# Attention into two mixture layers: the fp16 high parts written by ScalarE, and a router chain cut into eleven pieces

## Chip, cores and metric

The kernel runs on one core of a Trainium2 chip. The metric is device time in microseconds (us) of one execution; three executions of the kernel before gave a median of 1026.43 us (1021.26 to 1030.29).

## What is computed

The reference first runs a chunked attention over 4 batches, 8 heads, 768 positions and head size 64: each chunk of 32 queries sees its own 32 keys, 16 to the left, 8 to the right and 8 memory keys. The result, 3072 tokens of width 512, goes through a top-2 mixture of 8 experts with a noisy router, and then through a top-1 mixture of 8 other experts:

```
scores = 0.125 * q_c @ k_full.T ; a = softmax(scores) ; out[c] = a @ v_full
noisy = x @ w_gate + log1p(exp(x @ w_noise)) * noise
top2 = two largest of noisy ; weights = softmax over the two
out[token] += weight[k] * relu(x @ w1[e]) @ w2[e]       for its two experts e
second mixture: the one expert of largest logit, weight = softmax probability
```

## The kernel before

The tokens are worked in 24 tiles of 128 tokens (t = 0 to 23, `NT`). The attention loop in `build` (lines 1253 to 1302) runs 26 rounds, and the program gives each engine its instructions exactly in the order in which this loop writes them; each engine works its own queue in that order, and semaphores hold an instruction until its data is there. In round t the loop writes:

- `scores(t)`, lines 305 to 326: 32 matmuls `s` on TensorE (PE, L316), then on VectorE (DVE) a maximum `m` (L323) and a subtraction `d` (L325).
- `flip(t-1)`, lines 335 to 342: four transposes `pt` on PE, copied by ScalarE (ACT) into `et`.
- `exp(t)`, lines 328 to 333: three activations on ACT.
- pieces of the router chain, lines 1280 to 1282 (below).
- `values(t-2)`, lines 344 to 376: 32 matmuls `o` on PE (L356), then on DVE `r`, its reciprocal and the product `x` (L362, L363, L365), the fp16 cast of `x` (L369), which is the high part; GpSimd (POOL) subtracts to make the low part (L370). Both parts are stored to `X16` by a DMA on SyncE's queue (SP), behind the five loads of tile t+3 (L293).
- `spread(t)`, lines 295 to 303: two or four copies on POOL that fill the neighbour rows of the value tile.
- `turn(t-3)`, lines 378 to 384: eight transposes `xp` on PE of the two parts, copied by ACT into `xt` (L384).
- `logits(t-4)`, lines 386 to 392: eight small matmuls `lg` on PE.

The accumulators `o`, `pt` and `xp` have one buffer each, `s` has two; so `o(t-2)` can't start before DVE has finished `x(t-3)`, and `xp(t-3)` can't start before ACT has copied `xp(t-4)`. Five tile buffers (`LK`) hold the loaded inputs: the load of tile t+3 waits until PE has finished `o(t-2)`.

After every sixth tile the router of that batch is worked by the generator `route` (lines 394 to 495), whose `yield`s cut it into pieces; each `next(route)` writes one piece. Its parts are named here A (logits, exp, ln), B (noise, maximum of eight and its index, L408 to L419), C (one-hots, L422 to L436), D (`count` on PE, positions, L438 to L452), E (one-hot tables on DVE, L454 to L461), F (table matmuls on PE, L465, then table and gates, L467 to L484) and G (L487 to L494, middle batches only). A batch's chain begins at the end of rounds 9, 15 and 21; the fourth batch's chain is run in `tail()` by the `Driver`, one piece per step of the first mixture.

From round 14 on, 512 KB weight chunks are loaded ahead (`Weights`, four `stage` buffers). Rounds 24 and 25 each convert one chunk: ACT writes the fp16 high part (`high`, L127), DVE the low part (`low`, L128). Two more chunks follow (c0 to c3 in all) before the first expert's matmuls `ph` (L543) can run to the end of their first output tile. The first mixture then runs 15 groups of two or three tiles, with matmuls `ph` and `py` (L543, L554).

Of the kernel before, what the change touches and what calls it, by code (L numbers as in the profile page):

```python
# [10 lines left out]
AF = mybir.ActivationFunctionType  # L11
# [11 lines left out]
DM, F, E = 512, 1024, 8  # L23
# [199 lines left out]
def count(nc, g, pos, cnt, oh, carry=None):  # L223

    n = oh.shape[1]
    last = carry is None
    nc.tensor.matmul(pos, g.tri, oh, start=True, stop=False)
    for s in range(1, n):
        nc.tensor.matmul(pos[:, s:, :], g.ones, oh[:, :n - s, :], start=False, stop=last and s == n - 1)
    if not last:  # L230
        nc.tensor.matmul(pos, g.ones, carry[:, None, :].to_broadcast([128, n, E]), start=False, stop=True)
    if cnt is not None:
        for t in range(n):
            nc.tensor.matmul(cnt, g.ones, oh[:, t, :], start=(t == 0), stop=(t == n - 1))
# [20 lines left out]
class Attention:  # L255
# [88 lines left out]
    def values(self, t):  # L344
        nc, wk, g = self.nc, self.wk, self.g
        x = self.X[t % LK]
        y = self.ET.pop(t)
        o = self.ps.tile([128, 2, 512], F32, name="o")
        for a in range(2):
            for u in range(2):  # L350
                for ch in range(4):
                    i = (D + 1) * (4 * ch + 2 * a + u)
                    v = x[:, i:i + D + 1]
                    v = bass.AP(tensor=v.tensor, offset=v.offset, ap=[v.ap[0], [XV + (3 - 2 * ch) * VC, 2], v.ap[1]])
                    j = 64 * (ch % 2) + 32 * u
                    nc.tensor.matmul(o[32 * ch:32 * ch + 32, a, 130 * u:130 * u + 130],  # L356
                                     y[:, 2 * (ch // 2) + a, j:j + 32], v, start=True, stop=True)
        if t + LK < NT:
            self.load(t + LK)
        o = o[:, :, 0:260].rearrange("p a (h d) -> p a h d", h=4)  # L360
        r = wk.tile([128, 2, 4, 1], F32, name="r")
        nc.vector.tensor_scalar(r, o[:, :, :, D:D + 1], 1e-9, 1.0 / SX, op0=OP.add, op1=OP.mult)  # L362
        nc.vector.reciprocal(r, r)  # L363
        x = wk.tile([128, 2, 4, D], F32, name="x", bufs=2)
        nc.vector.tensor_tensor(x, o[:, :, :, 0:D], r.to_broadcast([128, 2, 4, D]), op=OP.mult)  # L365
        xp = x.rearrange("p b a d -> p (b a d)")
        w = g.rr.tile([128, 2, 4, 128], F16, name="x16", bufs=2)
        wf = w.rearrange("p a k q -> p (a k q)")
        nc.vector.tensor_copy(wf[:, :DM], xp)  # L369
        nc.gpsimd.tensor_tensor(wf[:, DM:], xp, wf[:, :DM], op=OP.subtract)  # L370
        y = self.XT[t] = g.rr.tile([128, 2, 4, 128], F16, name="xt", bufs=3)
        if t >= NT - 2:
            nc.sync.dma_start_transpose(out=y.rearrange("p a k q -> p (a k) q"), in_=wf)
        else:
            self.W[t] = w
        self.stores.append(nc.sync.dma_start(rows(g.X16, t), wf))
# [17 lines left out]
    def route(self, b):  # L394

        nc, g = self.nc, self.g
# [15 lines left out]
        i8 = rr.tile([128, TB, 8], U32, name="i8")  # L412
        for j in range(TB):
            V.max(m8[:, j, :], ny[:, j, :])
        for j in range(TB):
            V.max_index(i8[:, j, :], m8[:, j, :], ny[:, j, :])
        dd = rr.tile([128, TB, 2], F32, name="dd")
# [8 lines left out]
                        op=OP.is_equal)  # L426
        two = rr.tile([128, TB, E], F16, name="two")
        V.tensor_tensor(two, oh[:, :, 0, :], oh[:, :, 1, :], op=OP.add)

        vb = rr.tile([128, TB, 2], F32, name="vb")  # L430
        vr = rr.tile([128, TB, 2], F32, name="vr")
# [6 lines left out]
        pp = g.psr.tile([128, 512], F32, name="misc")  # L438
        p3 = pp[:, 0:TB * E].rearrange("p (t e) -> p t e", t=TB)
        count(nc, g, p3, None, two, g.carry)  # L440
        pr = rr.tile(sh, F32, name="pr")
        V.tensor_tensor(pr, oh, p3[:, :, None, :].to_broadcast(sh), op=OP.mult)
        pos = g.pos[:, ts, :]
        with nc.allow_low_precision("positions are integers"):
# [15 lines left out]
        ol, ov = onehots(nc, g, lo.rearrange("p t k -> p (t k)"), col.rearrange("p t k -> p (t k)"), g.slot,  # L460
                          eng=None)  # L461
        yield 6.5
        tp = pp[:, 128:128 + NC]
        for i in range(M):
            nc.tensor.matmul(tp, ol[:, :, i], ov[:, :, i], start=(i == 0), stop=(i == M - 1))  # L465
# [6 lines left out]
        V.tensor_tensor(full, full, tp, op=OP.add)  # L472
        V.tensor_tensor(gt[:, :, 1], gt[:, :, 0], dd[:, :, 0], op=OP.mult)
        V.tensor_tensor(g.T, g.T, full, op=OP.add)
        if b:

            n = NC if b == B - 1 else max(k // 128 + 8 * u for u, k in enumerate(LEAST[b]) if k)
            g.tabs.append(tables1(nc, g.c, g.T, n, f"t{b}"))
# [35 lines left out]
def rows(x, t):  # L514

    return x.rearrange("(u p t) d -> u p t d", u=2, t=M)[t // M, :, t % M]


def tables1(nc, pool, T, n, name, mem=None):

    V = nc.vector
    v, gi, xi, yi = mem or [pool.tile([128, n], F32 if u == "v" else I32, name=name + u) for u in "vgxy"]
    T = T[:, 0:n]
    V.tensor_scalar(gi, T, -1.0, 0.0, op0=OP.add, op1=OP.max)
    V.tensor_scalar(xi, gi, 1, None, op0=OP.arith_shift_right)
    V.tensor_scalar(v, T, 0.0, float(BIG), op0=OP.is_equal, op1=OP.mult)
    V.tensor_tensor(yi, gi, v, op=OP.add)
    return xi, gi, yi
# [686 lines left out]
def build(tc, xa, xb, xc, xd, xe, noise, wr, wg2, w1, w2, v1, v2, out):  # L1215
    nc = tc.nc
    with ExitStack() as top:
# [18 lines left out]
        def src(e):  # L1236
            v = (w1[e].rearrange("(p k) f -> p (k f)", k=4), w2[e].rearrange("(p k) d -> p (k d)", k=8))
            return lambda i, c: v[i][:, c * 1024:c * 1024 + 1024]

        with ExitStack() as ctx:  # L1240
            wk = ctx.enter_context(tc.tile_pool(name="wk", bufs=2))
            ld = ctx.enter_context(tc.tile_pool(name="ld", bufs=1))
            at = Attention(tc, g, (xa, xb, xc, xd, xe), ld, wk)
            at.ps = ctx.enter_context(tc.tile_pool(name="psa", bufs=1, space=PSUM))
            at.load(0)
            nc.scalar.preload_act_table_set("natural_log_exp_and_others")
            gates = at.gates(noise, wr)
            at.clear(0)
            constants(tc, g, ld)
            for t in range(1, LK):  # L1250
                at.load(t)
            route = None
            for t in range(NT + 2):
                if t + 1 < LK:
                    at.clear(t + 1)
                if t == 0:
                    next(gates)
                if t == 3:
                    at.wrh = next(gates)
                if t == 2:  # L1260
                    g.wide = g.c.tile([128, 128, M], F16, name="wide")
                    nc.vector.tensor_copy(g.wide, g.iota[:, 0:128, None].to_broadcast([128, 128, M]))
                    z = ld.tile([128, NT * E], F32, name="zero")
                    nc.vector.memset(z, 0.0)
                    for u in range(2):
                        nc.sync.dma_start(g.L.rearrange("(u p t) x -> u p (t x)", u=2, p=128)[u], z)
                    nc.sync.dma_start(g.G.rearrange("(p t) x -> p (t x)", p=128), z[:, 0:2 * NT])
                if t >= 14:
                    W.depth = min(W.depth + 1, 4)
                    if t == 14:  # L1270
                        for e in range(E):
                            W.add((1, e), src(e))
                    W.fill()
                if t < NT:
                    at.scores(t)
                if 0 < t <= NT:
                    at.flip(t - 1)
                if t < NT:
                    at.exp(t)
                if route and t < 25:  # L1280
                    for _ in range(2 if t in (17,22) else 1):
                        next(route, None)
                if t >= 2:
                    at.values(t - 2)
                if t < NT:
                    at.spread(t)
                if 0 <= t - 3 < NT - 2:
                    at.turn(t - 3)
                if t >= 4:
                    at.logits(t - 4)  # L1290
                if t >= 4 and (t - 4) % TB == TB - 1:
                    route = at.route((t - 4) // TB)
                    next(route)
                if t == 20:
                    m1 = Moe1(tc, g, dr)
                    m1.gather(0)
                if t == 22:
                    for b in range(m1.preps(0)):
                        m1.prep(0, b)
                if t >= 24 and W.may():  # L1300
                    W.high()
                    W.low(nc.vector)
            m1.gates(0)
# [224 lines left out]
```

## Time and profile before

| what | value |
| --- | --- |
| median of three runs | 1026.43 us |
| lowest, highest | 1021.26, 1030.29 us |
| the profiled execution | 1026.23 us |
| its span, first to last instruction | 1024.4 us |
| PE busy | 961.8 us, 94% |
| DVE, ACT, POOL busy | 498.4, 383.9, 480.8 us |

The span is 1.8 us shorter than the profiled execution's own time, and that execution is 0.2 us below the median. Times inside the program are counted from the start of the span. The shares are means over the whole program: PE is busy nearly all the time in the two mixtures, which begin near 147 us, while the attention in front of them has gaps on PE and a much busier DVE. What the change touches is nearly all in front of 215 us.

### The profile page before, as it was taken

The page shows a single profiled execution, that of the slowest core. Times are in us where ns is not written, and L with a number is a line of the kernel's source. Part 1 is how long each engine was busy: PE and PEld are TensorE (multiplying, and loading weights), DVE is VectorE, ACT ScalarE, POOL GpSimd, SP SyncE. Part 2 cuts the span into 40 slices and gives each one's busy share as a digit, 9 for nine tenths or more (in the row PEclk, how much of TensorE's full clock was granted, in tenths as well). Part 3 has the DMA queues.
Part 4 walks back from the last instruction along what each step waited for, and adds up shares of the span by engine and source line. Part 5 has one row for each costly group of instructions (what it writes and reads, how often), then busy time and mean ns, then how long its engine had stood idle before and what let it go on. Part 6 is the DMA issues. An engine that isn't in the chain of part 4 may idle for free.

```text
span 1024.4 us, 18828 instructions
## 1 busy us (share of the span) xinstructions
PE 961.8 (94%) x7303; PEld 573.0 (56%) x7303; DVE 498.4 (49%) x1028; ACT 383.9 (37%) x649; POOL 480.8 (47%) x484
## 2 busy tenths in 40 slices
PE   5898959999999999999999999999988998999998
PEld 4787845656545555455555555554564564555665
DVE  7689886642413443234233323584574265465511
ACT  2444445322323343244333333353323344454421
POOL 6765562343545454636455445335227245434321
PEclk9998989999999999999999999999989999999999
DMA  9999959744746686669657666499356689998720
GB/s 210 252 257 245 249 128 295 186 96 112 192 101 172 163 183 162 150 158 192 161 152 182 139 160 145 99 302 237 69 170 179 167 207 267 265 190 239 148 58 19
DMA packets 189219, 180.75 MB, mean 176 GB/s; under 512 B 152149, under 2 KB 153045, under 8 KB 188353
## 3 DMA queue, kind: packets, MB, share of 16 engines
q1 hardware_dynamic: 166736, 131.24, 54.2%
q0 software_dynamic: 21952, 48.07, 15.6%
q8 instruction: 60, 0.98, 0.4%
q14 instruction: 39, 0.31, 0.1%
q10 hardware_dynamic: 432, 0.15, 0.1%
HBM read 118.27 MB, written 39.53 MB: 154 GB/s over the span
## 4 chain that ended last, share of the span: by engine, by line
PE 43%; issue 13%; POOL 6%; DMA 4%; DVE 3%; ACT 1%; POOLq 0%; SPq 0%; ACTq 0%; DVEq 0%
PE ph L543 21%; PE py L554 20%; POOL x L1035 2%; DMA stage<-in_v_dram 2%; DMA xt<-x 2%; POOL out_dram L1054 1%; PE pr L733 1%; POOL xp L1007 1%; POOL gs L1007 1%; ACT w L127 1%; DVE w L128 1%; DMA xp<-Y,tbr 1%; DVE hT L546 0%; POOL L L657 0%; DMA xT<-xg 0%
## 5 line engine op out<-in xcount | busy, mean ns | idle before, releaser
L543 PE MATMUL ph<-xT,w 128*128 128x384 f16 (+3 forms) x2688 | 425.4, 318 | 20.0 <-DVE hT L546 9.8
L554 PE MATMUL py<-w,hT 128*128 128x512 f16 x1800 | 394.4, 379 | 0.9 <-ACT hT L545 0.6
L543 PEld LDWEIGHTS <-w 128*128 128x128 f16 x2688 | 262.6, 99 | 165.0 <-issue 25.1
L554 PEld LDWEIGHTS <-hT 128*128 128x128 f16 x1800 | 175.6, 98 | 208.5 <-ACT hT L545 1.1
L546 DVE SCALAR_TENSOR_TENSOR hT<-ph,hT 128x384 f16<-128x384 f32 (+3 forms) x224 | 115.6, 520 | 226.2 <-ACT hT L545 225.2
L128 DVE SCALAR_TENSOR_TENSOR w<-stage,w 128x1024 f16<-128x1024 f32 x128 | 167.8, 1315 | 70.7 <-ACT w L127 69.8
L545 ACT ACTIVATE hT<-ph 128x384 f16<-128x384 f32 (+3 forms) x224 | 103.4, 463 | 218.7 <-PE ph L543 216.4
L127 ACT ACTIVATE w<-stage 128x1024 f16<-128x1024 f32 x128 | 133.5, 1049 | 22.0 <-DMA stage<-in_v_dram 18.8
L654 ACT ACTIVATE y<-py,gs 128x512 f32<-128x512 f32 x48 | 33.0, 686 | 177.7 <-PE py L554 171.6
L675 DVE SCALAR_TENSOR_TENSOR x<-y,x 128x512 f16<-128x512 f32 x50 | 34.4, 688 | 124.0 <-ACT x L671 124.0
L657 POOL DMA_INDIRECT L<-l,t3y x43 | 45.0, 1045 | 105.1 <-DVE l L686 102.7
L657 POOL DMA_INDIRECT Y<-y,t3y x43 | 44.8, 1042 | 92.5 <-ACT y L654 81.1
L1054 POOL DMA_INDIRECT out_dram<-y,tbo x22 | 23.1, 1048 | 125.5 <-ACT y L1053 107.4
L611 POOL DMA_INDIRECT Y<-ol,late x48 | 57.8, 1204 | 16.4 <-issue 16.4
L316 PE MATMUL s<-x 128*64 128x64 f32 x768 | 49.7, 289 | 16.1 <-DMA x<-in_xe_dram 10.8
L316 PEld LDWEIGHTS s<-x 128*64 128x64 f32 x768 | 46.3, 208 | 17.5 <-POOL x L303 8.3
L1053 ACT ACTIVATE y<-py,gs 128x512 f32<-128x512 f32 x27 | 18.5, 686 | 93.2 <-PE py L554 62.9
L370 POOL TENSOR_TENSOR x<-x,x 128x512 f16<-128x512 f32 x24 | 29.5, 1228 | 47.3 <-DVE x L369 21.7
L585 POOL DMA_INDIRECT xg<-X,t3x x43 | 42.2, 980 | 15.1 <-issue 14.3
L585 POOL DMA_INDIRECT gs<-G,t3g x41 | 38.8, 946 | 12.5 <-issue 12.5
L303 POOL COPY x<-x 24x780 f32<-24x780 f32 x48 | 41.0, 854 | 4.4 <-issue 1.7
L1035 POOL TENSOR_TENSOR x<-xp 128x512 f32<-128x512 f32 x27 | 36.0, 1354 | 14.6 <-DVE xg L1038 9.9
(274 smaller groups left out, 712.7 us busy)
## 6 DMA issues: line engine op xcount, KB each, us to landing
stage<-in_w_dram SPq DMA_DIRECT2D x64, 512.0 KB, 4.1
stage<-in_v_dram SPq DMA_DIRECT2D x64, 512.0 KB, 5.3
x<-in_xa_dram SPq DMA_DIRECT2D x24, 286.0 KB, 5.5
X<-x SPq DMA_DIRECT2D x24, 256.0 KB, 4.9
x<-in_xd_dram SPq DMA_DIRECT2D x24, 194.0 KB, 7.2
x<-in_xb_dram SPq DMA_DIRECT2D x24, 188.5 KB, 7.0
x<-in_xc_dram SPq DMA_DIRECT2D x24, 184.0 KB, 5.5
x<-in_xe_dram SPq DMA_DIRECT2D x24, 96.5 KB, 5.5
```

Source lines behind the costliest of these rows:

```text
L127: nc.scalar.activation(hi, src, AF.Copy, scale=SW)
L128: return lambda v=nc.vector: v.scalar_tensor_tensor(lo, src, SW, hi, op0=OP.mult, op1=OP.subtract)
L303: self.nc.gpsimd.tensor_copy(x[p + 32:p + 56, d:d + 3 * VC], x[p:p + 24, s:s + 3 * VC])
L316: nc.tensor.matmul(s[o:o + 64, ch // 2, b], q[:, b, ch], k[:, b, 40 * ch:40 * ch + 64], start=True, stop=True)
L543: nc.tensor.matmul(p[:, :n], w1[:, a, k, f, :], xT[:, b, k, :n], start=(i == 0), stop=(i == 11))
L545: nc.scalar.activation(hT[:, 0, f, :n], p[:, :n], AF.Relu)
L546: nc.vector.scalar_tensor_tensor(hT[:, 1, f, :n], p[:, :n], 0.0, hT[:, 0, f, :n], op0=OP.max, op1=OP.subtract)
L554: nc.tensor.matmul(p[:m], hT[:, a, f, o:o + m], w2[:, c, f, :], start=(i == 0), stop=(i == 23))
L585: self.nc.gpsimd.indirect_dma_start(out=out, out_offset=None, in_=src, in_offset=IO(ap=idx, axis=0))
L611: st = nc.gpsimd.indirect_dma_start(out=self.Y, out_offset=IO(ap=idx[:, i:i + 1], axis=0), in_=z, in_offset=None, bounds_check=2 * N - 1, ...
L657: st = nc.gpsimd.indirect_dma_start(out=dst, out_offset=IO(ap=idx, axis=0), in_=src, in_offset=None, bounds_check=2 * N - 1, oob_is_err=False)
L1035: nc.gpsimd.tensor_tensor(s, x[:, :DM], x[:, DM:], op=OP.add)
```

## The change

The high part of every tile is written by an ACT copy in place of the DVE cast. `route` gets five more `yield 0.0`, which make eleven pieces of the six parts A to F (twelve with G), and the loop calls it at two places of a round: after `exp(t)` as before, and again between `turn(t-3)` and `logits(t-4)`. B becomes B1 (up to the maximum) and B2 (its index), C becomes C1 (one-hots) and C2, D becomes D1 (the `count` on PE) and D2 (positions), an empty piece follows E, and F becomes F1 (table matmuls, gates, table) and F2. In rounds 17, 22, 23 and 24 two pieces are written at the first place.

```
--- before.py
+++ after.py
@@ -366,7 +366,7 @@
         xp = x.rearrange("p b a d -> p (b a d)")
         w = g.rr.tile([128, 2, 4, 128], F16, name="x16", bufs=2)
         wf = w.rearrange("p a k q -> p (a k q)")
-        nc.vector.tensor_copy(wf[:, :DM], xp)
+        nc.scalar.activation(wf[:, :DM], xp, AF.Copy)
         nc.gpsimd.tensor_tensor(wf[:, DM:], xp, wf[:, :DM], op=OP.subtract)
         y = self.XT[t] = g.rr.tile([128, 2, 4, 128], F16, name="xt", bufs=3)
         if t >= NT - 2:
@@ -412,6 +412,7 @@
         i8 = rr.tile([128, TB, 8], U32, name="i8")
         for j in range(TB):
             V.max(m8[:, j, :], ny[:, j, :])
+        yield 0.0
         for j in range(TB):
             V.max_index(i8[:, j, :], m8[:, j, :], ny[:, j, :])
         dd = rr.tile([128, TB, 2], F32, name="dd")
@@ -426,6 +427,7 @@
                         op=OP.is_equal)
         two = rr.tile([128, TB, E], F16, name="two")
         V.tensor_tensor(two, oh[:, :, 0, :], oh[:, :, 1, :], op=OP.add)
+        yield 0.0
 
         vb = rr.tile([128, TB, 2], F32, name="vb")
         vr = rr.tile([128, TB, 2], F32, name="vr")
@@ -438,6 +440,7 @@
         pp = g.psr.tile([128, 512], F32, name="misc")
         p3 = pp[:, 0:TB * E].rearrange("p (t e) -> p t e", t=TB)
         count(nc, g, p3, None, two, g.carry)
+        yield 0.0
         pr = rr.tile(sh, F32, name="pr")
         V.tensor_tensor(pr, oh, p3[:, :, None, :].to_broadcast(sh), op=OP.mult)
         pos = g.pos[:, ts, :]
@@ -460,6 +463,7 @@
         ol, ov = onehots(nc, g, lo.rearrange("p t k -> p (t k)"), col.rearrange("p t k -> p (t k)"), g.slot,
                           eng=None)
         yield 6.5
+        yield 0.0
         tp = pp[:, 128:128 + NC]
         for i in range(M):
             nc.tensor.matmul(tp, ol[:, :, i], ov[:, :, i], start=(i == 0), stop=(i == M - 1))
@@ -472,6 +476,7 @@
         V.tensor_tensor(full, full, tp, op=OP.add)
         V.tensor_tensor(gt[:, :, 1], gt[:, :, 0], dd[:, :, 0], op=OP.mult)
         V.tensor_tensor(g.T, g.T, full, op=OP.add)
+        yield 0.0
         if b:
 
             n = NC if b == B - 1 else max(k // 128 + 8 * u for u, k in enumerate(LEAST[b]) if k)
@@ -1278,7 +1283,7 @@
                 if t < NT:
                     at.exp(t)
                 if route and t < 25:
-                    for _ in range(2 if t in (17,22) else 1):
+                    for _ in range(2 if t == 17 or t > 21 else 1):
                         next(route, None)
                 if t >= 2:
                     at.values(t - 2)
@@ -1286,6 +1291,8 @@
                     at.spread(t)
                 if 0 <= t - 3 < NT - 2:
                     at.turn(t - 3)
+                if route and t < 25:
+                    next(route, None)
                 if t >= 4:
                     at.logits(t - 4)
                 if t >= 4 and (t - 4) % TB == TB - 1:
```

PE in round 17, whose route is the second batch's. Before, from the scores of tile 17 (`s`) on:

```order
L316 MATMUL s<-x_90 64x64 x16
L340 MATMUL pt<-ident,e 128x128 x4
L227 LDWEIGHTS tri
L227 MATMUL misc<-two,tri 128x48
L229 LDWEIGHTS ones
```

And the same place of PE's queue now:

```order
L316 MATMUL s<-x_90 64x64 x16
L340 MATMUL pt<-ident,e 128x128 x4
L356 MATMUL o<-x_88,et 32x130 x16
L383 LDWEIGHTS x_1633
L383 MATMUL xp<-ident_117,x_1633 128x128
```

Before, the count (`misc<-two`, part D) stood in front of `o` of tile 15; now `o` and the transposes `xp` go first and the count stands behind them.

ACT at the end of the attention, from the copy `et` of tile 23 in round 24 to the weights' high parts (`w_71`). Before:

```order
L342 ACTIVATE et<-pt 128x512
L384 ACTIVATE xt<-xp 128x1024
L127 ACTIVATE w_71<-stage 128x1024 x2
L247 DMA wg2f<-in_wg_dram 128x32
L250 ACTIVATE wg_2518<-wg2f 128x32
L127 ACTIVATE w_71<-stage 128x1024 x2
```

And now:

```order
L342 ACTIVATE et<-pt 128x512
L369 ACTIVATE x_2429<-x 128x512
L384 ACTIVATE xt<-xp 128x1024
L127 ACTIVATE w_71<-stage 128x1024
L369 ACTIVATE x_2499<-x 128x512
L127 ACTIVATE w_71<-stage 128x1024
L247 DMA wg2f<-in_wg_dram 128x32
L250 ACTIVATE wg_2538<-wg2f 128x32
L127 ACTIVATE w_71<-stage 128x1024 x2
```

The high parts of tiles 22 and 23 now stand in front of `xt` and of the first two weight chunks on ACT's queue.

DVE at the same place, from `r` of tile 22 on. Before:

```order
L362 TENSOR_SCALAR r<-o 128x8
L363 RECIPROCAL r<-r 128x8
L365 TENSOR_TENSOR x<-o,r 128x512
L369 CAST x_2429<-x 128x512
L128 SCALAR_TENSOR_TENSOR w_71<-stage,w_71 128x1024
L362 TENSOR_SCALAR r<-o 128x8
L363 RECIPROCAL r<-r 128x8
L365 TENSOR_TENSOR x<-o,r 128x512
L369 CAST x_2479<-x 128x512
L128 SCALAR_TENSOR_TENSOR w_71<-stage,w_71 128x1024
```

And now:

```order
L362 TENSOR_SCALAR r<-o 128x8
L363 RECIPROCAL r<-r 128x8
L365 TENSOR_TENSOR x<-o,r 128x512
L472 RECIPROCAL gt<-dd 128x6
L474 TENSOR_SCALAR full<-misc 128x64
L475 TENSOR_SCALAR gt<-gt 128x6
L476 TENSOR_TENSOR full<-full,misc 128x64
L477 TENSOR_TENSOR gt<-gt,dd 128x6
L478 TENSOR_TENSOR T<-T,full 128x64
L128 SCALAR_TENSOR_TENSOR w_71<-stage,w_71 128x1024
L362 TENSOR_SCALAR r<-o 128x8
L363 RECIPROCAL r<-r 128x8
```

The casts are gone, and F1's six table instructions, which stood among the first expert's work before, now stand in front of the first low part.

## Rows read from the trace of the kernel before

**Rows 1.** The page's first part: busy time of each engine.

```profile
PE 961.8 (94%) x7303; PEld 573.0 (56%) x7303; DVE 498.4 (49%) x1028; ACT 383.9 (37%) x649; POOL 480.8 (47%) x484
```

**Rows 2.** Stages by window: length; busy PE, PEld, DVE, ACT, POOL; clock, DMA share, GB/s.

```profile
40.00:60.00 20.00, 20.00 (x386) 17.91 (x388) 13.38 (x31) 10.69 (x24) 14.25 (x16) 1.00 1.03 267
...
61.37:94.13 32.76, 30.10 (x527) 26.29 (x523) 30.18 (x90) 14.74 (x34) 19.16 (x21) 0.95 0.95 249
94.13:119.68 25.55, 20.77 (x361) 18.29 (x357) 21.80 (x81) 9.26 (x20) 11.28 (x13) 0.87 1.03 254
119.68:130.34 10.66, 8.92 (x171) 7.76 (x168) 8.92 (x37) 5.53 (x14) 9.58 (x11) 1.00 0.89 226
130.34:152.30 21.96, 12.62 (x198) 9.11 (x195) 20.37 (x45) 8.86 (x14) 13.48 (x12) 0.80 0.45 116
...
100.00:105.00 5.00, 4.24 (x71) 3.65 (x70) 3.80 (x17) 0.97 (x1) 0.68 (x2) 0.50 1.04 253
```

**Rows 3.** Timeline of PE, rounds 9, 10, 17, 18: start, duration, instruction, idle before.

```profile
52.67 2.07 PE L316 MATMUL s<-x 128*64 128x64 f32 x32
57.02 2.08 PE L316 MATMUL s<-x 128*64 128x64 f32 x32
...
100.76 0.20 PE L227 MATMUL misc<-two,tri 128*128 128x48 f16 x1 [4.00 <-DVE two L428]
...
101.07 1.96 PE L356 MATMUL o<-x,et 128*32 128x130 f32 x32
...
106.69 1.09 PE L356 MATMUL o<-x,et 128*32 128x130 f32 x32
```

**Rows 4.** PE's waits from 61 to 130.4 us: in total, times, longest.

```profile
PE misc L227 <- DVE two L428: 4.0, 1, 4.0
PE xp L383 <- POOL x L370: 2.3, 5, 1.2
```

**Rows 5.** The cast's line on DVE, by window: length, busy, clock, DMA.

```profile
61.37:130.34 68.97, 5.75 (x12) 0.93 0.97 247
```

**Rows 6.** Timeline of DVE and POOL in round 13: x, cast, low part.

```profile
74.28 0.69 DVE L365 TENSOR_TENSOR x<-o,r 128x512 f32<-128x512 f32 x1
...
75.01 0.43 DVE L369 CAST x<-x 128x512 f16<-128x512 f32 x1
...
75.67 1.16 POOL L370 TENSOR_TENSOR x<-x,x 128x512 f16<-128x512 f32 x1 [2.03 <-DVE x L369]
```

**Rows 7.** ACT's same copy in the first mixture: duration in ns, min/median/max.

```profile
L671 ACT ACTIVATE x<-y x50: 629/629/635, 172.3 to 716.9; 128x512 f16<-128x512 f32 x50
```

**Rows 8.** Timeline of DVE: one router instruction, with and without POOL copies beside it.

```profile
66.72 0.90 DVE L425 TENSOR_TENSOR oh<-iota,eid 128x96 f16<-128x96 f16 x1
...
130.81 0.26 DVE L425 TENSOR_TENSOR oh<-iota,eid 128x96 f16<-128x96 f16 x1
```

**Rows 9.** Timeline of ACT and DVE in rounds 24 and 25.

```profile
140.38 1.02 ACT L384 ACTIVATE xt<-xp 128x1024 f16<-128x1024 f16 x1 [3.33 <-PE xp L383]
...
141.30 1.99 ACT L127 ACTIVATE w<-stage 128x1024 f16<-128x1024 f32 x2
...
143.27 0.69 DVE L365 TENSOR_TENSOR x<-o,r 128x512 f32<-128x512 f32 x1
...
144.34 1.22 DVE L128 SCALAR_TENSOR_TENSOR w<-stage,w 128x1024 f16<-128x1024 f32 x1
...
146.63 0.69 DVE L365 TENSOR_TENSOR x<-o,r 128x512 f32<-128x512 f32 x1
...
147.70 1.22 DVE L128 SCALAR_TENSOR_TENSOR w<-stage,w 128x1024 f16<-128x1024 f32 x1
...
152.30 6.60 PE L543 MATMUL ph<-xT,w 128*128 128x256 f16 x37 [0.31 <-DVE w L128]
```

**Rows 10.** Timeline of PE in the first mixture: the table, two waits.

```profile
158.74 1.61 PE L465 MATMUL misc<-ov,ol 128*128 128x64 f16 x12
...
178.98 3.23 PE L543 MATMUL ph<-xT,w 128*128 128x256 f16 x28 [1.90 <-DMA xT<-xg]
...
205.18 8.20 PE L543 MATMUL ph<-xT,w 128*128 128x384 f16 x48 [1.66 <-DVE onov L1160]
```

More of the change, by code (lines that the diff above doesn't have):

```diff
@@ L368, in values @@
         wf = w.rearrange("p a k q -> p (a k q)")
-        nc.vector.tensor_copy(wf[:, :DM], xp)
+        nc.scalar.activation(wf[:, :DM], xp, AF.Copy)
         nc.gpsimd.tensor_tensor(wf[:, DM:], xp, wf[:, :DM], op=OP.subtract)
@@ L414, in route @@
             V.max(m8[:, j, :], ny[:, j, :])
+        yield 0.0
         for j in range(TB):
@@ L428, in route @@
         V.tensor_tensor(two, oh[:, :, 0, :], oh[:, :, 1, :], op=OP.add)
+        yield 0.0
         vb = rr.tile([128, TB, 2], F32, name="vb")
@@ L440, in route @@
         count(nc, g, p3, None, two, g.carry)
+        yield 0.0
         pr = rr.tile(sh, F32, name="pr")
@@ L462, in route @@
         yield 6.5
+        yield 0.0
         tp = pp[:, 128:128 + NC]
@@ L474, in route @@
         V.tensor_tensor(g.T, g.T, full, op=OP.add)
+        yield 0.0
         if b:
@@ L1280, in build @@
                 if route and t < 25:
-                    for _ in range(2 if t in (17,22) else 1):
+                    for _ in range(2 if t == 17 or t > 21 else 1):
                         next(route, None)
@@ L1288, in build @@
                     at.turn(t - 3)
+                if route and t < 25:
+                    next(route, None)
                 if t >= 4:
```

## The prediction

> **What bounds the kernel now.** Read the page's first part first. PE is busy 94% of the span and DVE 49% [rows 1], so the program is PE's, and relief on DVE can pay only where PE stands still. The change lies in the attention, so read the stages next. In rounds without a router piece PE has no gap: 20.00 of 20 us, at full clock (the first window) [rows 2], and scores of two tiles start 4.35 us apart (57.02 less 52.67) [rows 3]. The windows behind it begin and end where the scores of tiles 11, 17, 21 and 23 start. Six rounds take 32.76 us there where six of 4.35 would take 26.1, and DVE is busy 30.18 us of them, 92%: with router pieces DVE sets the pace. The next four take 25.55 us with DVE at 21.80, 85%: there something else waits too. In the timeline of PE it is one place: in round 17 part C on DVE and the count on PE stand in one round, PE waits 4.00 us for `two`, and `o` of tile 15 is queued behind it. That `o` then takes 1.96 us where another takes 1.09 [rows 3]; the granted clock is 0.50 in those five microseconds, the lower of the two levels (1.2 against 2.4 GHz; the last window) [rows 2].
>
> Last look at the DMA column, which the change doesn't touch. It stands at 1.03 in the PE-bound stage with 267 GB/s, and at 0.95, 1.03 and 0.89 in the three router stages with 249, 254 and 226 GB/s [rows 2]. The loads are close to their own limit while DVE holds the rounds back.
>
> **The change part by part. The casts.** 12 casts lie between 61.37 and 130.34 us, 5.75 us of DVE time, 0.48 each [rows 5]; an undisturbed one takes 0.43 [rows 6]. On ACT the same copy, 128x512 from f32 to f16, takes 0.629 us in the first mixture [rows 7]. ACT has room (14.74 of 32.76 us busy) [rows 2]. But the low part on POOL comes later: `x` ended at 74.97 and POOL started at 75.67, 0.70 behind it [rows 6]. With ACT it is 0.63 and two handovers of some 0.15 (0.70 less the cast's 0.43 is 0.27 for two), about 0.93, that is 0.25 later. PE waits for this low part already, 2.3 us in five rounds [rows 4]; five times 0.25 is 1.2 us given back. In the nine rounds before, DVE is busy 13.38 of 20 us and POOL's part isn't needed until a round later; I cost them at nothing, and 0.25 a round, 2.3 us, if that cover is gone.
>
> Rounds 11 to 16: six casts less, 6 x 0.48 = 2.9, less 1.2, gain 1.7. Their D and E and F stay in the same rounds, so nothing else shifts.
>
> **Round 17.** The count goes behind `o` and `xp`, so the 4.00 us wait no longer holds them, nor the 0.87 us that `o` lost at the low clock. What is late next is DVE itself: 21.80 us of work less four casts (1.9) is 19.9; at the 92% share of the stage before that takes 21.6 us in place of 25.55. Gain 3.9, not 4.9.
>
> Rounds 21 and 22: two casts, 0.96, less 0.25, gain 0.7. By the engines the scores of tile 23 start 1.7 + 3.9 + 0.7 = 6.3 us earlier.
>
> **The loads behind it.** The three stages moved 249 x 32.76 + 254 x 25.55 + 226 x 10.66, 17.06 MB, and nearly all must land before tile 23 can be scored; weight chunks are among it. At the 254 GB/s of the stage with DMA share 1.03 that takes 67.1 us of today's 68.97, a gain of 1.8; at the 267 of the PE-bound stage 63.9, a gain of 5.1. Both rows show a saturated queue, so neither is excluded; I take the middle, **3.4 us**, and keep 1.8 and 6.3 as ends.
>
> **Rounds 24 and 25, where it is given back.** The first expert's matmuls run freely from 152.30, when the low part of chunk c3 is there [rows 9]. Before, ACT had `xt` of tile 21 at 140.38 and both high parts from 141.30 on, done before `x` of tile 22 (143.27 to 143.96); the low part c0 on DVE began at 144.34, 0.38 behind `x`. Now ACT's queue is: high part of tile 22, which waits for `x`, then `xt` (1.02), then the high part of c0 (1.99 for two, 1.0 each). DVE can begin c0 only 0.63 + 1.02 + 1.0 and handovers of 0.15 behind `x`: 2.8 in place of 0.38, 2.4 later. F1, now in front of c0 on DVE, lies under this wait: its table takes PE 1.61 us [rows 10] from the end of part E on, 1.2 us before the end of `x`. Behind c0 stand `r` and `x` of tile 23, so they shift too. Then the high part of tile 23 and that of c1 stand before DVE's c1: 0.63 + 1.0 + 0.1 against 0.38 (147.32 to 147.70), 1.4 later. One cast in front of part E is gone, 0.4. Together 2.4 + 1.4 - 0.4, **3.4 us given back**. As little as 1.0 if only one chunk counts; 5.0 if POOL's copies also hold F1's instructions.
>
> **The first mixture.** The third batch's table leaves PE at 158.74, 1.61 us, but the second group waits at 178.98 for transposed tokens 1.90 us [rows 10], and that wait takes up what PE wins; what DVE wins by it is some 0.7. In the fourth batch five more pieces are five more steps of `tail()`, so its table moves from between `py` matmuls to behind the first `ph` of the next group, and the count of overflow, for which PE waits 1.66 at 205.18, to two `ph` steps later, with ACT's and DVE's halves of `ph` (0.5 each) in front. I set +0.7 against -0.7: **nothing**, with ends -1.6 and +3.
>
> **Sum.** -3.4 + 3.4 + 0 = 0.0 us. All of it is against the profiled execution: 1026.23 us, of which 1024.4 is the span; the median of the runs is 0.2 above. I predict **1026.2 us**.
>
> **A rule weighed.** With POOL's copies beside it the one-hot instruction took 0.90 us, without them 0.26 [rows 8]. The Trainium skill, page "SBUF — State Buffer", section "Who interferes with whom", says why: a VectorE instruction with two SBUF inputs and a GpSimd instruction that reads SBUF keep each other out for the whole instruction. This trace agrees. It speaks against the first place of a round, where the one-hots, the noise and the tables still meet POOL's copies, and for the second, where DVE works while POOL waits for ACT's copy. Two instructions of D2 would escape so in each of two batches, about 0.6 us each by the difference of these two rows; the sum by it would be near 1024. I leave it out of the sum because the loads cap that stage.
>
> **Rivals.** *The loads keep up.* For it: 267 GB/s were reached with PE never waiting. Against: the share of 1.03 in the stage in question. Then the engines' 6.3 us count whole, and if the chunks cost only 1.0 and PE keeps the table's 1.6, the time is 1026.2 - 6.9 = 1019.3. Chance 0.2.
>
> *ACT's queue becomes PE's wait; slower.* Place: every router round. ACT's copy `xt` stands behind the high part, which stands behind `x`, and `xp` has one buffer: PE can't start the next `xp` before 0.63 + 1.02 + 0.15 = 1.8 us behind `x`, while its `o` lasts 1.09. It decides from the point at which `x` ends less than 0.7 us before `o` starts, the state in which DVE is late. Price up to 0.7 a round, 0.4 in the mean over 12 rounds, 4.8; the gain of 3.4 turns to a loss of 1.4, with 5.0 given back in the last rounds: 1026.2 + 6.4 = 1032.6. For it: DVE is late in just these rounds (92%). Against: without the cast it is less so. Chance 0.16.
>
> *The tail's new order costs.* The fourth batch's later table delays the gathers of the group behind it, and PE waits for the overflow count at a worse place: +3, 1029.2. Against: that group starts some 30 us later. Chance 0.12.
>
> **How the numbers follow.** The forecast itself has 0.5; its own range is 1021 to 1031, from the ends 1.8 to 6.3, 1.0 to 5.0 and the runs' scatter. The range of 8 in 10 reaches a little past the rivals' times and that scatter (5 us to either side in three runs): 1016 to 1034. A measurement here can tell about 1%, 10.3 us. Faster by more than that needs the first rival and 4 us of scatter or more: 0.2 x 0.35 and a rest, 0.09. Slower by more needs the second and as much: 0.16 x 0.3 and a rest, 0.07. Within 1%: 0.84.
>
> **What would show it.** Right, step by step: no wait of PE for `two`; scores of tile 17 to 21 in about 22 to 24 us; PE's waits for POOL's low part or ACT's `xt` longer than 2.3 us; the DMA share at 1.0 or above from 61 us to the scores of tile 23; the low part of c0 some 2.8 us behind `x` of tile 22; the start of free `ph` matmuls within 3 us of 152.30. Wrong: tile 23 scored more than 6 us earlier with the DMA share falling, or the free `ph` matmuls from 147 us or earlier, or from 156 and later.

## The result, and the profile after

Seven runs of each kernel: 1033.76 us after (1029.0 to 1036.54) against 1026.98 before (1021.26 to 1030.29). The ratio is 1.0067, 95% interval 1.004 to 1.0094: slower by some 7 us, where 1026.2 was predicted. The profiled execution took 1036.54 us, its span is 1034.8.

The page's first part, engine by engine: DVE is busy 483.2 us where it was 498.4 [rows 1], so the casts did leave it; the relief bought no time.

```profile
PE 964.2 (93%) x7303; PEld 572.5 (55%) x7303; DVE 483.2 (47%) x1004; ACT 397.1 (38%) x673; POOL 475.1 (46%) x484
```

The windows that answer to [rows 2], again between the starts of the scores of tiles 11, 17, 21 and 23 (start and end; then busy time and instructions of PE, PEld, DVE, ACT, POOL; granted clock, DMA share, GB/s):

```profile
40.00:60.00 20.00, 20.00 (x384) 17.91 (x386) 11.27 (x25) 13.92 (x29) 14.17 (x16) 1.00 1.03 264
61.48:93.08 31.60, 28.45 (x527) 25.23 (x524) 28.14 (x99) 17.65 (x40) 20.32 (x22) 1.00 1.03 256
93.08:121.54 28.46, 20.69 (x356) 18.03 (x357) 17.67 (x63) 11.91 (x25) 12.96 (x14) 0.94 1.02 254
121.54:131.54 10.00, 10.00 (x172) 8.58 (x169) 6.06 (x21) 6.06 (x14) 6.94 (x8) 0.83 0.78 210
```

DVE's share of the middle stage is 62% (17.67 of 28.46), where it was 85%, and yet the stage is 2.9 us longer. PE's waits in these rounds say why; they answer to [rows 4]:

```profile
PE s L316 <- DMA x<-in_xe_dram: 4.6, 2, 2.4
PE s L316 <- DMA x<-in_xd_dram: 2.8, 1, 2.8
PE misc L493 <- DVE carry L489: 2.0, 1, 2.0
PE xp L383 <- ACT xt L384: 0.7, 2, 0.4
PE misc L227 <- DVE two L429: 0.5, 1, 0.5
PE o L356 <- POOL x L303: 0.2, 1, 0.2
```

The wait for `two` went from 4.0 to 0.5 us. In its place PE waits 7.4 us for loads, and 2.0 for `carry`: the second batch's last piece now stands in the same round as the piece before it.

Most of the loss lies elsewhere. In the timeline of PE (start, duration, line, operation, idle time before it and what ended it) this is the third group of the first mixture:

```profile
202.85 2.11 PE L548 MATMUL ph<-xT,w 128*128 128x384 f16 x12
204.80 1.61 PE L469 MATMUL misc<-ov,ol 128*128 128x64 f16 x12
...
208.69 0.17 PE L240 MATMUL lg<-wg,xt 128*128 128x16 f16 x1 [2.10 <-DVE l L691]
...
209.31 0.17 PE L240 MATMUL lg<-wg,xt 128*128 128x16 f16 x1 [0.27 <-DVE l L691]
...
209.52 6.81 PE L548 MATMUL ph<-xT,w 128*128 128x384 f16 x24
216.16 0.17 PE L1154 MATMUL misc<-carry,ones 128*128 128x8 f16 x1
218.94 3.58 PE L548 MATMUL ph<-xT,w 128*128 128x384 f16 x12 [2.61 <-DVE onov L1165]
...
230.36 4.91 PE L559 MATMUL py<-w,hT 128*128 128x512 f16 x22
```

Behind the first 12 `ph` stands the fourth batch's table, behind it three gatings of the second router (`lg`, eight small matmuls each) in a row. The second of them waits 2.10 us until DVE has read the first (`l`), and DVE reads it only behind the chain that the table feeds:

```profile
206.59 0.18 DVE L472 RECIPROCAL gt<-dd 128x6 f32<-128x6 f32 x1
206.69 0.18 DVE L474 TENSOR_SCALAR full<-misc 128x64 f32<-128x64 f32 x1
...
208.39 0.16 DVE L489 TENSOR_TENSOR carry<-carry,cm 128x8 f16<-128x8 f16 x1
208.47 0.17 DVE L691 TENSOR_REDUCE l<-lg 128x8 f32<-128x16 f32 x1
```

Then 24 `ph` take 6.81 us and 12 take 3.58. The windows of these stretches give the granted clock (third number from the right): 0.50, the lower of its two levels (1.2 against 2.4 GHz), right behind the pause, and 0.58 behind the next.

```profile
206.40:209.50 3.10, 0.74 (x25) 0.61 (x21) 2.27 (x15) 0.00 (x0) 0.99 (x1) 0.81 0.49 87
209.50:211.00 1.50, 1.50 (x12) 0.73 (x9) 0.17 (x1) 0.00 (x0) 0.09 (x1) 0.50 0.34 98
211.00:216.20 5.20, 5.20 (x21) 2.58 (x20) 0.56 (x1) 0.49 (x1) 3.98 (x5) 0.60 0.37 111
218.94:222.50 3.56, 3.56 (x18) 1.81 (x18) 2.68 (x8) 0.00 (x0) 2.14 (x2) 0.58 0.56 103
```

In all, that group's `ph` stage took 27.51 us (202.85 to 230.36) where it took 16.24 before (205.18 to 221.42). The stage ahead of it, `py` of the second group, gave 4.1 back (10.36 where it was 14.44): the table (1.4), two gatings (0.8 with their wait) and the count of overflow (1.8, of which 1.66 is its wait [rows 10]) left it. Before, that stage read:

```profile
195.92 1.60 PE L465 MATMUL misc<-ov,ol 128*128 128x64 f16 x12
197.35 2.77 PE L554 MATMUL py<-w,hT 128*128 128x512 f16 x12
199.96 0.17 PE L240 MATMUL lg<-wg,xt 128*128 128x16 f16 x1
...
200.57 0.17 PE L240 MATMUL lg<-wg,xt 128*128 128x16 f16 x1 [0.27 <-DVE l L686]
...
221.42 15.70 PE L554 MATMUL py<-w,hT 128*128 128x512 f16 x72
```

Two gatings stood in a row there too, but 12 `py` stood between the table and them: DVE had finished the table's chain at 199.60, and PE waited 0.27 us for `l` in place of 2.10.

### The profile page after: what moved, and what is told of

It reads as the page before. It is cut to its first block, busy times and chain, and to the rows that moved or that the text cites. A ratio compares the mean times of both kernels' runs of the same rounds, so it can differ in the third digit from the quotient of the medians.

```text
span 1034.8 us, 18834 instructions
## 1 busy us (share of the span) xinstructions
PE 964.2 (93%) x7303; PEld 572.5 (55%) x7303; DVE 483.2 (47%) x1004; ACT 397.1 (38%) x673; POOL 475.1 (46%) x484
## 4 chain that ended last, share of the span: by engine, by line
PE 43%; issue 13%; POOL 6%; DMA 4%; DVE 4%; ACT 1%; POOLq 0%; SPq 0%; DVEq 0%; ACTq 0%
PE ph L548 21%; PE py L559 20%; POOL x L1040 2%; PE pr L738 1%; POOL out_dram L1059 1%; DMA stage<-in_v_dram 1%; POOL xp L1012 1%; POOL gs L1012 1%; DVE w L128 1%; DMA xt<-x 1%; DMA xp<-Y,ter 1%; DMA xp<-Y,tbr 1%; DVE hT L551 0%; ACT w L127 0%; DMA xT<-xg 0%
```

## The experiments

Landmarks of each profile, from PE's timeline, in us. The first column of times is the start of the scores of tile 23. The last but one runs from the first `ph` of the second group (behind its wait for `xT`) to the first `ph` of the fourth: the stretch that the tail's order touches. Ratios are to the kernel before on the same chip, with 95% intervals.

| run | scores 23 | first ph | group 2 | group 4 | 2 to 4 | ratio |
|---|---|---|---|---|---|---|
| before | 130.34 | 147.42 | 178.98 | 236.96 | 57.98 | 1 |
| after | 131.54 | 150.29 | 180.80 | 245.90 | 65.10 | 1.0067 (1.004 to 1.0094) |
| e1 old tail | 127.26 | 147.60 | 178.49 | 236.45 | 57.96 | 1.0001 (0.9976 to 1.0026) |
| e2 new tail only | 133.73 | 150.96 | 183.55 | 247.59 | 64.04 | 1.0083 (1.0054 to 1.0113) |
| e3 cast only | 128.48 | 145.77 | 178.89 | 237.10 | 58.21 | 0.999 (0.9969 to 1.0011) |
| e5 pieces, old tail | 131.47 | 151.17 | 181.82 | 240.08 | 58.26 | 1.0026 (1.0004 to 1.0049) |
| e7 count late | 127.20 | 145.62 | 177.96 | 236.79 | 58.83 | 0.9997 (0.9971 to 1.0023) |
| e8 count out | 127.81 | 147.54 | 180.10 | 246.03 | 65.93 | 1.0059 (1.0027 to 1.009) |
| e15 gates apart | 126.94 | 146.04 | 176.91 | 236.86 | 59.95 | 1.0017 (0.9987 to 1.0048) |
| e9 waits out | 128.74 | 146.84 | 177.81 | 235.24 | 57.43 | 0.9988 (0.9971 to 1.0006) |
| e12 all mended | 124.17 | 143.50 | 176.06 | 233.47 | 57.41 | 0.9946 (0.9925 to 0.9968) |
| e10 weights late | 124.52 | 143.37 | 177.18 | 235.42 | 58.24 | one run |
| e11 gate slots | 127.64 | 145.96 | 178.07 | 240.99 | 62.92 | 1.0065 (1.0037 to 1.0093) |
| e13 before, weights late | 131.78 | 148.50 | 181.16 | 240.39 | 59.23 | 1.0000 (0.9978 to 1.0022) |
| e14 e12, cast on DVE | 129.84 | 149.11 | 178.84 | 236.31 | 57.47 | 0.9993 (0.9977 to 1.0008) |
| e16 no pause | 127.94 | 146.89 | 177.47 | 239.68 | 62.21 | 1.0021 (0.9991 to 1.0050) |

**Tail or attention?** The first four kernels take the change apart. e1 keeps all of it but the added pieces of the fourth batch, at five places of `route`:

```diff
-        yield 0.0
+        if b < B - 1:
+            yield 0.0
```

> The changed kernel with the fourth batch's route cut as it was before (its five added pieces end at batch 3), so that behind the attention PE's order is that of the kernel before, but for the third batch's table, which stays in round 24. Theory T (the tail's new order is the loss): the third group's first-layer stage goes back from 27.5 us to some 16 us and the py stage ahead of it takes its table back, net 6.8 us less: within 2 us of 1027 + 2, so 1027 to 1030, and 5 to 8 us under the changed kernel. Theory A (the attention's rounds 17 to 25 are the loss): no more than 2 us under the changed kernel, 1031 to 1034. In both the attention's own landmarks stay: scores of tile 23 near 131.5, free first-layer matmuls near 157.

Measured: 1026.56 us, level with before. The whole loss is gone. Its scores of tile 23 came at 127.26, not near 131.5 as expected; the last section takes that up.

e2 is its mirror, the kernel before with the pieces of the fourth batch alone, at those places:

```diff
+        if b == B - 1:
+            yield 0.0
```

> The kernel before with nothing but the five added pieces in the fourth batch's route; the attention is word for word that of before. Theory T: 5 to 8 us slower than before, 1032 to 1035, with the wait of PE for the gating's l, the wait for onov above 2 us and a low granted clock between them in the third group. Theory A: within 1.5 us of before.

Measured: 1034.96 us; its profile has the wait for `l` (2.11) and for `onov` (2.68). So the fourth batch's five pieces alone make the kernel as slow as the whole change does. Theory A, that the attention is the loss, is out.

e3 is the kernel before with the cast on ACT alone:

```diff
-        nc.vector.tensor_copy(wf[:, :DM], xp)
+        nc.scalar.activation(wf[:, :DM], xp, AF.Copy)
```

e5 is e1 with this line turned back: the pieces of the other batches alone.

> The kernel before with the high part on ACT and nothing else. If ACT's queue is the price (xt behind the cast, low part 0.25 us later a round, weight chunks later in rounds 24 and 25): free first-layer matmuls 1 to 4 us later than 152.3 and the time 1 to 4 us above before. If the relief of DVE counts: scores of tile 23 some 1.5 to 3 us earlier than 130.3 and the time 0 to 3 us below before. If the loads hold both: scores of tile 23 within 1 us of 130.3.

> The pieces at two places in the attention's batches only, high part on DVE as before, the fourth batch as before. If the places are what loses in the attention (count of the second batch's carry in front of tile 21, table in front of o of tile 23): scores of tile 21 with a wait for carry of 1 us or more, table wait of 2 us or more in front of o of tile 23, free first-layer matmuls at 154 to 157, time 1 to 4 us above before. If the cast is: free first-layer matmuls at 149 to 152 and the time 1 to 4 us below before. The wait of 4.0 us for two in round 17 is gone in both.

Measured: e3 1025.8, no difference that shows, with the scores of tile 23 some 1.9 us earlier and the first `ph` 1.7; e5 1028.17, slower by a quarter of a per cent. In e5 PE waits 3.72 us for `ov` in front of `o` of tile 23 and 1.60 for `carry`; the 4.0 for `two` became 1.92, not nothing. Both halves of the change in the attention are worth little by themselves, and together nothing (e1).

**Which move of the tail?** e7 is e1 with only the count moved back, e8 the changed kernel with the count moved out:

```diff
             m1.ready = True
-            yield 2.0
+            yield 5.0
```

(12.0 in e8.)

> The changed kernel with the old route of the fourth batch (as in the run of the old tail), and of the new tail's two moves only one: the count of overflow goes from in front of the third group's first ph to behind 24 of them; its table stays between the py matmuls. If this move carries the loss (PE waits for onov in the middle of a stage and runs on at the low clock): 3 to 6 us above the run of the old tail, 1030 to 1033. If the table and the three gatings behind it carry it: within 1.5 us of the run of the old tail, 1025 to 1028.

> The changed kernel, and of the new tail's two moves only the other: the table stays behind the first 12 ph of the third group with three gatings in a row behind it, but the count of overflow goes on to the start of that group's py matmuls. If table and gatings carry the loss: PE still waits some 2 us for the gating's l and runs at the low clock behind it; 3 us or less under the changed kernel, 1031 to 1034. If the count carries it: 4 us or more under it, 1027 to 1030.

Measured: e7 1026.55, no loss; e8 1033.92, nothing won back. It is the table with its gatings. In e7 PE waits 2.61 us for `onov` amid the stage and runs on at full clock; in e8 PE waits 2.11 for `l`, and the clock falls. The windows, of e7 first (the pause and what follows), then of e8:

```profile
206.30:209.02 2.72, 0.11 (x3) 0.04 (x1) 1.92 (x8) 0.49 (x1) 2.11 (x3) 1.00 0.77 181
209.02:213.00 3.98, 3.98 (x28) 2.42 (x28) 3.32 (x11) 0.49 (x1) 3.04 (x3) 1.00 0.74 183
```

```profile
206.40:209.47 3.07, 0.69 (x22) 0.56 (x19) 2.23 (x15) 0.00 (x0) 0.99 (x1) 0.81 0.49 87
209.47:212.00 2.53, 2.53 (x15) 1.18 (x13) 0.17 (x1) 0.00 (x0) 0.96 (x1) 0.50 0.33 104
212.00:215.00 3.00, 3.00 (x11) 1.48 (x10) 0.56 (x1) 0.49 (x1) 2.34 (x3) 0.50 0.32 89
```

**The pause or the place?** e11 gave the gatings six slots of their accumulator tile (PSUM) in turn, so that none should wait for the one before it.

```diff
-                lg = g.psr.tile([128, TB, 32], F32, name="lg")[:, 0]
+                if g.lgn % TB == 0 and g.lgt is None:
+                    g.lgt = g.psr.tile([128, TB, 32], F32, name="lg")
+                lg = g.lgt[:, g.lgn % TB]
+                g.lgn += 1
```

> The changed kernel, order and all, but the second router's gatings take turns over six slots of their PSUM tile, so that a gating no longer waits until VectorE has read the one before it. If the pause behind the late table is the price (2.1 + 0.3 us of waiting, and the low clock that follows it): no wait for l, full clock in the third group's first-layer matmuls up to the wait for onov, and 4 to 8 us under the changed kernel, 1026 to 1030. If the table's later place costs by itself (gathers later, or the clock falls at the table anyway): 2 us or less under it, 1032 to 1034.

Measured: 1032.57 us, ratio 1.0065 (1.0037 to 1.0093), but the edit missed its aim: the wait for `l` is still there, 2.10 us. Slots of one tile did not release the writer. So e11 says nothing on the price of the pause; e15 takes the pause away by order, and e16 the register load of the count as well (moved as in e9 below):

```diff
-            while not self.ready:
+            while not self.ready or group is not None and self.dr.now < self.free:
                 yield 1.0
+            self.free = self.dr.now + 2.0
...
+    free = 0.0
```

> The changed kernel, its late table and its late count where they are, but the three gatings of the second router no longer in a row behind the table: a gating waits for at least two units of the planner's clock behind the one before, so that ph matmuls stand between them. If the pause behind the table and the low clock after it are the price: no wait for l, full clock in the third group up to the count, and 4 to 8 us under the changed kernel's 1033.8, 1026 to 1030. If the table's later place costs by itself: 2 us or less under it, 1032 to 1034.

> The run with the gatings apart, and the register load of the overflow count some steps behind the count, so that no wait of PE is left in the third group although table and count stay at the changed kernel's places. If the pauses are the price: 1.5 to 4 us under the run with the gatings apart, and level with before or a little under it, 1024 to 1028. If the places are: within 1.5 us of the run with the gatings apart.

These two ran on a chip on which the kernel before takes 1035.11 us, so only ratios compare, and the changed kernel was not run on it. e15 stands at 1.0017, against 1.0067 of the changed kernel: 0.0050, 5.1 us of 1027. Its interval and the changed kernel's overlap a little, but the trace says the same. With the table and the count still at the changed kernel's places, the stage takes 22.36 us (198.96 to 221.32) in place of 27.51, a difference of 5.15:

```profile
200.91 1.61 PE L469 MATMUL misc<-ov,ol 128*128 128x64 f16 x12
202.57 4.06 PE L548 MATMUL ph<-xT,w 128*128 128x384 f16 x24
206.46 0.17 PE L1157 MATMUL misc<-carry,ones 128*128 128x8 f16 x1
209.42 0.17 PE L240 MATMUL lg<-wg,xt 128*128 128x16 f16 x1 [2.79 <-DVE onov L1168]
209.64 4.06 PE L548 MATMUL ph<-xT,w 128*128 128x384 f16 x24
```

24 `ph` take 4.06 us again. One wait for `l` is left, 1.37 us in front of a later gating. e16 moved a wait rather than removing it: without the load PE runs on to the next gating and waits there 3.88 us, for DVE again (`late`), with the clock at 0.50 behind it. Ratio 1.0021 (0.9991 to 1.005), level with e15 within these intervals, though its profile has 2.3 us more from group 2 to 4. The order that the planner (`Driver`) gives is tight in that stage; what is taken out at one place shows at the next.

**Do the loads bind the attention?** e9 is e1 with three waits taken out by order, e10 is e1 with the weight loads later, e12 has both and e11's slots, e13 is before with the later loads, and e14 is e12 with the cast on DVE.

```diff
-    g.nov = nc.values_load(n[0:1, 0:1], min_val=0, max_val=56)
+    g.onov = n
...
-                if route and t < 25:
+                if route and (t < 24 and t != 20 or t == 25):
                     next(route, None)
...
             blanks.extend(m1.blank(r2.late))
+            yield 6.0
+            g.nov = nc.values_load(g.onov[0:1, 0:1], min_val=0, max_val=56)
```

```diff
-                if t >= 14:
+                if t >= 20:
                     W.depth = min(W.depth + 1, 4)
-                    if t == 14:
+                    if t == 20:
```

(The second is that of e12 to e14; e10 has 22 in place of 20.)

> The run of the old tail with three waits of PE taken out by order alone: the register load of the overflow count goes some steps behind the count (1.65 us of wait in front of the third group), the second batch's last piece goes from the second place of round 20 to the first of round 21 (wait of 2.0 us for carry), and the third batch's table goes behind o of tile 23 (wait of 2.7 us for ov in front of it). If PE's waits in the attention count as such: the sum of 1.65, 2.0 and some 2 of the 2.7, 4 to 6 us under the old tail's 1026.6, 1021 to 1023. If the loads set the end of the rounds and the weight chunks the start of the first group: only the 1.65 and about 1 more, 1024 to 1025.

> The run of the old tail with the weight stage's first loads begun in round 22 instead of 14, so that four loads of 512 KB (2.1 MB, 8 us at 255 GB/s) leave rounds 14 to 21. If the loads bind those rounds: no wait of PE for x of a tile between 60 and 130 us, and scores of tile 23 at 120 to 124, 4 to 10 us earlier than in the two runs of these rounds (127.3 and 131.5). If the engines bind them: scores of tile 23 within 2 us of 127.3. In both the first group starts late, since its weights come later; the whole time says nothing.

> The run with PE's waits taken out by order (old tail, count's load later, last piece of the second batch in round 21, third table behind o of tile 23), with the six gating slots, and with the weight stage's loads begun in round 20. If the loads bound rounds 14 to 21: scores of tile 23 at 122 to 126 and 3 to 6 us under that run's 1024.9, 1019 to 1022. If the weights' later arrival takes it back in the first group: no more than 1 us under it, 1024 to 1026.

> The kernel before with nothing but the weight stage's loads begun in round 20 instead of 14. If VectorE holds rounds 11 to 22 of the kernel before, as the prediction has it, the loads were not what it waited for: scores of tile 23 within 1.5 us of 130.3, time within 1.5 us of before. If the loads held them too: scores of tile 23 at 124 to 128 and 2 to 5 us under before, 1022 to 1025.

> The run with everything mended, with the high part back on VectorE. If relief of VectorE counts once the loads don't bind: scores of tile 23 some 3 us later (12 casts of 0.48 less 0.25 each for the longer way) and 1 to 4 us above that run. If the weight chunks behind ACT's queue take it back in the last rounds: within 1 us of it.

Measured: e9 1024.85, ratio 0.9988 (0.9971 to 1.0006), so no gain clear of the scatter: PE still waits for tiles (2.09, 2.03 and 2.20 us at tiles 17 to 19), and `o` of tile 23 now waits 4.26 for `x` in place of the table, as its second expectation had it. e10 (one run): no wait for a tile from 60 us on, scores of tile 23 at 124.52, 2.7 earlier than in e1, less than the 4 expected; the first group did not start late either, and the time was 1021.72 us. e12: 1020.36, ratio 0.9946, faster than both kernels. PE's waits of e12 between 60 and 130 us:

```profile
PE misc L227 <- DVE two L430: 3.0, 2, 1.7
PE misc L473 <- DVE ov L520: 1.1, 1, 1.1
PE xp L383 <- POOL x L370: 1.0, 2, 0.6
PE xp L383 <- ACT xt L384: 0.3, 1, 0.3
```

No load is among them; the wait for `two` is back. e13: ratio 1.0000 (0.9978 to 1.0022), scores of tile 23 at 131.78: later loads win the kernel before nothing, so DVE was its limit. The loads are near theirs there too: in e2, whose rounds are those of before, PE waits 4.4 us for loads and tile 23 comes at 133.73. e14: 1024.17, 0.9993 (0.9977 to 1.0008), scores of tile 23 at 129.84, 5.7 us later than in e12: with the loads out of the way the cast on ACT is worth 3.8 us, as its first expectation had it, though by more in the rounds and less behind them. So each needs the other: later loads alone 0 (e13), cast and pieces alone 0 (e1), and with the mended order 0.9988 (e9), all but the cast 0.9993 (e14), all together 6 us. No run takes the added pieces out of e12, so their share of it is not shown.

## Why the prediction was wrong, point by point

**What bounds the kernel: right.** DVE holds the router rounds of the kernel before (e13: later loads alone change nothing), with the loads close behind, and PE holds the rest.

**The step that failed is "the first mixture: nothing", ends -1.6 and +3.** It named both moves of the fourth batch, the table behind the first `ph` and the count two steps on, and set +0.7 for them, without a working, against the 0.7 that DVE was to win by the third batch's table. What it left out is what else is queued there. The second router's gatings are held back until the fourth batch's route is done (`ready`); five pieces later three of them are due at once, in a row behind the table, and share one accumulator tile, which DVE empties only behind the table's chain. In that stage (+11.3 us) stand: the table 1.6, the pause and gatings 3.1, the count with its wait 2.8, and the low clock 2.75 + 1.47 (6.81 against 4.06, 3.58 against 2.11), 11.7 in all. That is 0.4 more than the stage grew, and half of it is a gating: two stood between the `ph` before, and besides the three only one does now. Against it 4.1 were given back by the stage ahead. The difference, 7.2, is within 0.1 of what the table of landmarks shows (65.10 less 57.98); e2's is 6.1. So the term set at nothing measured some +7, beyond its end of +3.

**The rival "the tail's new order costs" was the answer**, with a chance of 0.12 and a price of +3, less than half of what was measured. Its place was right. Its count moved late costs nothing that shows (e7); its table, said to delay the gathers, costs by the gatings and the clock behind it. The price needed two things that could be read beforehand: what is queued behind the moved instruction on PE, and what DVE had in front of the read it waits for.

**Rounds 11 to 23, -3.4: right in size, by six profiles of seven.** The seven kernels with these rounds as changed (after, e1, e7, e8, e11, e15, e16) have the scores of tile 23 at 126.94 to 127.94, but for the changed kernel's own profile, 131.54. Before had 130.34 (and 133.73 with the same rounds in e2), so 2.4 us or more were won by these profiles, and the one profile that the result shows is the odd one. The split was wrong. Between the scores of tiles 11 and 17 the seven take 28.99 to 31.60 us where before took 32.76, a gain of 1.2 to 3.8 (1.7 forecast). Between those of tiles 17 and 21 they take 25.51 to 28.46 where before took 25.55, so "Gain 3.9" and the sign "22 to 24 us" came in none: waits for loads and `carry` took the place of the wait for `two`, and even e10 and e12, without load waits, take 24.65 and 24.11. "The loads behind it" is shown: PE's waits for tiles in all seven, none in e10 and e12. The wait for `two` fell as argued; the wait for `carry` in front of tile 21, 1.0 to 2.2 us, was not foreseen.

**Rounds 24 and 25, +3.4: right in size, one mechanism missed.** From the scores of tile 23 to the start of the free `ph` the seven take 25.15 to 27.07 us where before took 21.96, 3.2 to 5.1 more; to the first `ph` it is 18.32 to 20.34 against 17.08. The changed kernel's own profile has its free `ph` from 157.01, past the 156 that was to count as wrong; the six others have it from 152.40 to 154.33. The low part of c0 starts 2.56 behind the end of `x` of tile 22 in the changed kernel (2.8 predicted), that of c1 1.65 behind that of tile 23 (1.7):

```profile
144.61 0.69 DVE L365 TENSOR_TENSOR x<-o,r 128x512 f32<-128x512 f32 x1
...
147.86 1.22 DVE L128 SCALAR_TENSOR_TENSOR w<-stage,w 128x1024 f16<-128x1024 f32 x1 [0.44 <-ACT w L127]
...
149.50 0.69 DVE L365 TENSOR_TENSOR x<-o,r 128x512 f32<-128x512 f32 x1
151.84 1.33 DVE L128 SCALAR_TENSOR_TENSOR w<-stage,w 128x1024 f16<-128x1024 f32 x1 [1.64 <-ACT w L127]
```

F1 on DVE did lie "under this wait": DVE still stood idle 0.44 us in front of c0. But on PE its table stands in front of `o` of tile 23, which starts 0.69 us behind the end of `x` of tile 22, where it was 0.14 before. After, then before:

```profile
144.25 1.61 PE L469 MATMUL misc<-ov,ol 128*128 128x64 f16 x12 [3.28 <-DVE ov L515]
...
145.99 1.96 PE L356 MATMUL o<-x,et 128*32 128x130 f32 x32
```

```profile
144.10 1.96 PE L356 MATMUL o<-x,et 128*32 128x130 f32 x32 [3.64 <-DVE x L365]
```

With the table behind `o` (e9) the wait only changed its name, 4.26 us for `x`: DVE's work in those two rounds sets their length.

**The rule weighed** held; what was forecast from it held for the one-hots and not for D2. `oh` takes 0.92 us at 66.97 in the changed kernel, where it meets POOL's copies, and 0.26 at 97.24, where POOL stands idle; before it took 0.90 and 0.88. But D2's slow instructions did not escape: `vr` took 0.77 at 72.90 before and takes 1.13 at 73.07 now, and `vi` of the third batch takes 1.01 at 139.53, since POOL's subtractions for the low part run beside them there (1.16 us each from 73.01 and 139.35). What was saved bought nothing by itself that shows, as the sum had assumed.

**ACT's queue as PE's wait** did not come: 0.7 us for `xt` in these rounds and none for POOL's low part, so the forecast's own sign, more than 2.3 us of these waits, failed too. **The loads keep up** did not come either; e12, with the loads later and the order mended, shows some of what it would have given.

## What to carry to other kernels

A piece more in a chain that a planner steps moves everything that waits for the chain's end. List, for each engine, what is queued behind the moved instructions and what becomes due at the same step; short pieces that share a buffer cost pauses when they come together. And where two resources are both near their limit, as VectorE and the loads here, relief of one can show nothing until the other is relieved too: change them in one run before either is given up.

## What the runs showed of the hardware

A pause of PE of 3.1 us with 0.7 us of narrow matmuls in it, behind 1.6 us of a table's narrow matmuls, was followed by the low clock (0.50); one of 2.7 us between wide matmuls was not (1.00, e7). Nor does the same pause do the same each time: behind the wait for the count, 2.6 to 2.7 us, the clock was 0.58 in the changed kernel and 1.00 in e11, where the low clock cost 1.7 us in all (24 `ph` in 5.6 us, the next 12 in 2.11). What decides is not shown. The Trainium skill, page "TensorE: Matmul & The Clock Gate", section "HAM oscillation — how this bites in real kernels", warns that a wait for data can leave PE at its lower clock when the next stretch starts; the changed kernel shows it for waits for VectorE's results, at 4.2 us for 36 matmuls, and e7 shows that not each pause of nearly that length does.

The saturated DMA queue does not give the same rate in each execution. From the scores of tile 11 to those of tile 21, with the same rounds and a DMA share of 1.02 to 1.03, the changed kernel's profile moved 256 and 254 GB/s, that of e1 263 and 284:

```profile
62.36:92.78 30.42, 28.04 (x527) 24.99 (x524) 27.00 (x93) 17.65 (x40) 20.42 (x23) 1.00 1.03 263
92.78:118.29 25.51, 21.04 (x357) 18.39 (x357) 19.24 (x67) 11.69 (x25) 13.55 (x14) 0.87 1.02 284
```

Their scores of tile 23 lie 4.3 us apart, of the size of the runs' scatter; PE's waits for loads, 7.4 us against 4.1, make up 3.3 of it. Where loads bind, one profile is not enough to size a term of 3 us.
